# A second level of products over pairs of batches in the second layer of an attention and MLP kernel

## The chip, the cores and the metric

The kernel runs on one core of a Trainium2 chip. The metric is the device time of one execution in microseconds, as the median of several runs. All arithmetic is in float32; each 128-row float32 matmul of the program shows up as two matmul and two weight-load instructions in the trace.

## The reference, cut to what matters

```python
# q, k, v: (8 batches, 12 heads, 448 rows, 64);  w_in: (768, 2048);  w_out: (2048, 768)
q_n, k_n = rmsnorm(q, g_q), rmsnorm(k, g_k)          # x / sqrt(mean(x*x) + 1e-6) * g
attn = softmax(q_n @ k_n.T / 8)
x = (attn @ v)                                       # heads side by side: (8*448, 768)
h = x @ w_in
out = (h - tanh(h)) @ w_out                          # (3584, 768)
```

The weights come in as float64 and are rounded on the chip at the start.

## The kernel before

**Layout.** Everything is kept transposed: an activation tile has 128 features on the partitions and the 448 rows of one batch along the free dimension. A batch of the input of the first layer is six such tiles (`xT`, one for each pair of heads), its hidden activations are one tile of 16 blocks of 128 features (`gT`, `CF` = 16), its output six blocks.

**The two layers.** Batches 1 to 7 compute both layers with one level of the Winograd form of Strassen's scheme: rows are halved (2 x 224, `HS`), the inner and the outer features too, and seven half-size products replace eight. The weights' seven combinations are made once, during batch 0, and kept in scratch DRAM (`w_in_dram`, `w_out_dram`); from there they are loaded again for each batch into a ring of six slots in SBUF (`ring_load`, five ahead of use). The activations' combinations are `tt` (first layer, four GpSimd subtractions of 128x224 for a pair of `xT` tiles) and `tg` (second layer, `factors` at L838 to L840 and L872). Products come in the order `ORDER = (1, 5, 6, 2, 3, 7, 4)`; 2, 3 and 7 add to the PSUM banks of 1, 5 and 6, so that a bank is read out, added to by a product two later, and read again. Three PSUM banks (`mm`) serve the products in turn. `hidden(b)` is the first layer: four sets of seven products of six matmuls each; its results are read out by ScalarE and VectorE (L845 to L861), ScalarE takes the tanh (L827) and VectorE or GpSimd subtracts it (L828, "shrink"). `project(b)` is the second layer: three sets of seven products of eight matmuls. Batch 0 is different: its second layer is plain, 96 matmuls of 448 columns (L969), since the weights are still being rounded.

**Stores.** `store` transposes an output block in 32x32 pieces on VectorE into a buffer `th` (L886), of which there are two (ScalarE's tanh uses the same two), and after a few products SP issues its four transfers to DRAM (L891, `step_out`).

**Attention.** A step `s` is one pair of heads of one batch; there are 48. From step 13 on, a slot begins with a visit: TensorE computes the scores of step s+1 and the values of step s in 32-column pieces (L542, L608, L596), ScalarE takes the exponentials, and the result is divided into `xT` (L722 to L727). The helpers of later steps follow: for step s+1 VectorE adds up the exponentials (L573, L579, L586), transposes and reduces them (`fold` L683, `fold_rest` L690), ScalarE gathers the pieces (L698), VectorE and ScalarE spread the sums (`spread_sums`, `turn_sums`); for steps s+2 and s+3 the norms of q and k are made (`square_blocks`, `norm_blocks` L484, `meet_blocks`, and a power of -1/2 on GpSimd, L499), q and k are scaled (L506) and transposed (L516, L520), and `load_blocks` (L473) loads step s+4.

**Order.** There is no scheduler: each engine runs its instructions in the order in which the program issues them. The layers are a generator that yields after every matmul with a nominal time; `run(ns)` advances it. A slot runs the visit, then takes the list `work` of 14 points and advances the layers by an equal stretch before each point and after the last. `gap_ns` sets the length: before the change every slot from step 12 on gets a sixth of the two layers of one batch. The layers work on batch b-1 while the attention works on batch b, so the layers of batch 7 stand alone at the end.

Of the kernel before, what the change touches and what calls it, by code (L numbers as in the profile page):

```python
# [144 lines left out]
def bounded_path(tc, ctx, q, k, v, moe_w_in, moe_w_out, out, g_col, ident, ones, half_ones, neg_half, early):  # L145
# [32 lines left out]
    SETS = CF // 4  # L178
    ORDER = (1, 5, 6, 2, 3, 7, 4)
# [18 lines left out]
    gp = pool("gp", bufs=1)  # L198
    wp_stack = ctx.enter_context(ExitStack())
# [14 lines left out]

    def load(s, names):
        b, hp = steps[s]
        for name in names:
            src = {"q": q, "k": k, "v": v}[name]
            if s == 0 and name != "v":
                t = early[name]  # L220
            else:
                shape = [CP, 2, NCH, D] if name == "q" else [P, NCH, 2, D] if name == "k" else [P, 2, NCH, D]
                t = nat.tile(shape, F32, name=f"{name}_nat", bufs=3 if name == "v" else 2)
                fetch(nc, name, t, src[b, 2 * hp : 2 * hp + 2], in_order(s))
            loaded[name, s] = t
# [8 lines left out]
    BLOCKS = {1: 0, 2: 1, 4: 2, 7: 3, 5: 4, 6: 5, 3: 6}  # L234
    w_out_dram = scratch.tile([P, 7, HC, HF, P], F32, name="w_out")
# [151 lines left out]
    def ring_slot():  # L387
# [4 lines left out]
    ring_steps = [  # L392
        (b, layer, j, p)
        for b in range(1, B)
        for layer, count in ((0, SETS), (1, HC))
        for j in range(count)
        for p in ORDER
    ]
    ring_tiles = {}

    def ring_load(to):

        for n in range(len(ring_tiles), min(to, len(ring_steps))):
            b, layer, j, p = ring_steps[n]
            t = ring_tiles[ring_steps[n]] = ring_slot()
            if layer == 0:
                assert kept[1] > j
                nc.sync.dma_start(out=t[:, : 2 * HALF], in_=w_in_dram[j, p])
            else:
                nc.sync.dma_start(out=t, in_=w_out_dram[:, BLOCKS[p], j].rearrange("p f d -> p (f d)"))  # L410

# [53 lines left out]
    def load_blocks(s):  # L465
        b, hp = steps[s]
        t = loaded["qk", s] = late["blocks"].tile([P, 2, NJ, BL], F32, name="qk_nat", bufs=2)
        for i, src in enumerate((q, k)):
            for h in range(2):
                rows = src[b, 2 * hp + h].rearrange("(j t) (m d) -> m t j d", t=BL, d=BL)  # L470
                for m in range(2):
                    r = (2 * h + m) * BL
                    nc.sync.dma_start(out=t[r : r + BL, i], in_=rows[m])  # L473
# [19 lines left out]
    def power_blocks(s):  # L493
# [4 lines left out]
        normed["rr", s] = mine  # L498
        nc.gpsimd.tensor_tensor(  # L499
# [202 lines left out]
    def spread_sums(s):  # L702

        acc = whole[s]
        total = late["blocks"].tile([2 * BL, NJ], F32, name="sum_all")
        nc.vector.reduce_sum(total, acc.rearrange("p g j -> p j g"), axis=AX.X)
        nc.vector.reciprocal(total, total)
        wide = whole[s] = late["blocks"].tile([2 * BL, NJ, BL], F32, name="sum_w")
        nc.scalar.copy(out=wide, in_=total[:, :, None].to_broadcast([2 * BL, NJ, BL]))

    def turn_sums(s):

        wide = whole[s]
        rs = whole[s] = late["blocks"].tile([2 * BL, S], F32, name="rs_T")
        nc.vector.transpose(out=rs, in_=wide.rearrange("p j k -> p (j k)"))

    def divide(s, av):
        b, hp = steps[s]
        rs = whole.pop(s)
        x = xT[b, hp] = xp.tile([P, S], F32, name="xT")  # L720
        if s >= FOLDED:
            nc.scalar.copy(out=x, in_=av[0][:, :S])  # L722
            nc.vector.tensor_tensor(out=x, in0=x, in1=av[1][:, :S], op=ALU.add)  # L723
        for m in range(2):
            rows = slice(m * D, (m + 1) * D)
            if s >= FOLDED:
                nc.vector.tensor_tensor(out=x[rows], in0=x[rows], in1=rs, op=ALU.mult)  # L727
                continue
            for n in range(2):
# [6 lines left out]
        if hp < HC:  # L736
            return
        c = hp - HC
        if c == 0:
            tt[b] = tp.tile([P, 3, HC, HS], F32, name="tt", bufs=1)  # L740
        eng = nc.vector if b == 0 and c == HC - 1 else nc.gpsimd
        x11, x12, x21, x22 = (xT[b, r][:, n : n + HS] for r in (c, hp) for n in (0, HS))
        t1, t2, t4 = (tt[b][:, i, c] for i in range(3))
        eng.tensor_tensor(out=t1, in0=x12, in1=x11, op=ALU.subtract)
        eng.tensor_tensor(out=t2, in0=x22, in1=t1, op=ALU.subtract)  # L745
        eng.tensor_tensor(out=x12, in0=x22, in1=x12, op=ALU.subtract)
        eng.tensor_tensor(out=t4, in0=x21, in1=t2, op=ALU.subtract)
# [15 lines left out]
    def products(b, layer, count, width, depth, moving, done_with):  # L763
# [8 lines left out]
        def product(j, p, bank, first):  # L772
# [27 lines left out]
            for fn in now:  # L800
                fn()

# [9 lines left out]
    def hidden(b):  # L812

        g = late["g"] = gp.tile([P, CF, S], F32, name="gT")
        t2 = late["tg"].tile([P, 3, HF, HS], F32, name="tg") if b else None
        late["t"] = t2
        x = [xT.pop((b, c)) for c in range(CD)]
        t = tt.pop(b)
# [3 lines left out]
            4: lambda c: t[:, 2, c], 5: lambda c: t[:, 0, c], 6: lambda c: t[:, 1, c], 7: lambda c: x[c][:, high],  # L822
# [7 lines left out]
        def done_with(j):  # L830
# [11 lines left out]
            def use(p, bank):  # L842
                v = view(bank)
                if p == 1:
# [15 lines left out]
                elif p == 4:  # L860
                    nc.vector.tensor_tensor(out=s1, in0=v, in1=s1, op=ALU.add)  # L861

                    if b and j == SETS - 1:
                        factors()

                    def rest():
                        shrink(down, low, s1, nc.gpsimd)
                        if b and j < SETS - 1:
                            factors()
                        if b:  # L870
# [9 lines left out]
    def store(b, n, y):  # L880
# [15 lines left out]
        late["out"].append([2, issue])  # L896

    def step_out(by=1):
        for entry in late["out"]:
            entry[0] -= by  # L900
        while late["out"] and late["out"][0][0] <= 0:
            late["out"].pop(0)[1]()

# [35 lines left out]
    def project_first(b):  # L939
# [39 lines left out]
        late["tg"] = pool("tg", bufs=1)  # L979
        late["blocks"] = pool("blocks", bufs=1)  # L980

    def mlp():
        late["todo"], late["keep"], late["out"] = [], [], []
        for b in range(B):
            yield from hidden(b)
            yield from project(b) if b else project_first(b)
        for fn in late["todo"]:
            fn()
        step_out(2)
# [14 lines left out]
    O_NS = 4 * HS / ENGINE_NS * 7 * HC * HF  # L1004

    def gap_ns(s):
# [3 lines left out]
        return (H_NS + O_NS) / (4 * NP)  # L1010
# [72 lines left out]
    def slot(s):  # L1083
# [18 lines left out]

        def scale_or_turn():
            if first:
                turn(s + 2, sc_bank(), sc_bank())
            else:
                scale_blocks(s + 2)

        work = (
            ((rows, scale_or_turn),),  # L1110
            ((rows and not first, lambda: turn_blocks(s + 2, 0)), (first, lambda: load_blocks(s + 3))),
            ((rows and not first, lambda: turn_blocks(s + 2, 1)), (has(s + 4), lambda: load_blocks(s + 4))),
            ((following, lambda: add(s + 1, False)), (ahead and not first, lambda: square_blocks(s + 3))),
            ((following, lambda: add_third(s + 1)),),
            ((ahead and not first, lambda: norm_blocks(s + 3)),),
            ((following, lambda: add_last(s + 1)), (ahead and not first, lambda: meet_blocks(s + 3))),
            ((folded, lambda: fold(s + 1)),),
            ((folded, lambda: fold_rest(s + 1)), (first, lambda: square_blocks(s + 3))),
            (
                (folded, lambda: gather(s + 1, 0)), (ahead and not first, lambda: power_blocks(s + 3)),  # L1120
                (first, lambda: norm_blocks(s + 3)),
            ),
            ((folded, lambda: gather(s + 1, 1)), (first, lambda: meet_blocks(s + 3))),
            ((folded, lambda: spread_sums(s + 1)), (first, lambda: power_blocks(s + 3))),
            (),
            ((folded, lambda: turn_sums(s + 1)),),
        )
# [364 lines left out]
```

## Time and profile before

| | us |
|---|---|
| median of 3 runs | 1376.66 (1376.35 to 1377.57) |
| the profiled execution | 1375.42 |
| its span, first to last instruction | 1373.5 |
| TensorE matmul busy | 1344.5 |
| VectorE, ScalarE, GpSimd busy | 888.6, 551.1, 555.5 |

The granted clock of TensorE was 0.997 of full speed over the span. The span has three parts: up to 283 us the weights are rounded, the first batches' attention runs, and batch 0 goes through its layers; from 283 to 1217 us slots of 26.81 us follow each other; from 1217 to 1366 us the layers of batch 7 run alone. In the profile's lines "PE" is TensorE, "PEld" its weight loads, "DVE" VectorE, "ACT" ScalarE, "POOL" GpSimd and "SP" the engine that issues nearly all transfers. A line "L791 ... mm<-gT,w_f" is an instruction of line 791 that writes `mm` from `gT` and `w_f`.

### The profile page before, as it was taken

Reading aid. Unit: us, or ns where it says so; the run is one execution under the profiler, and the core shown is the slowest. Engines: PE = TensorE matmul, PEld = TensorE weight load, DVE = VectorE, ACT = ScalarE, POOL = GpSimd, SP = SyncE. Lnnn points to the kernel's source line nnn. Section 1 sums busy time; section 2 is a strip of 40 time slices with the busy share of each in tenths; the row PEclk is TensorE's granted clock in tenths of the full one; section 3 lists DMA queues with packets and bytes.
Section 4 is the critical chain, followed back from the end, with each engine's and each line's share of the span. In section 5 each row is a group of like instructions: output and inputs, shape, how many; then the busy total and the mean of one; then the engine's idle time right before and its main releaser. Section 6 shows DMA issues by size and latency. Waiting matters only on the chain.

```text
span 1373.5 us, 29906 instructions
## 1 busy us (share of the span) xinstructions
PE 1344.5 (98%) x11840; PEld 1126.3 (82%) x11840; DVE 888.6 (65%) x1378; ACT 551.1 (40%) x1314; POOL 555.5 (40%) x345
## 2 busy tenths in 40 slices
PE   7988999999999999999999999999999999999997
PEld 3466854479988998898899889889988998999997
DVE  5999989747855775666765578557765677533311
ACT  7855654344433444334433444334443344211100
POOL 4756665233632355315543336323463155302300
PEclk9999999999999999999999999999999999999999
DMA  7879889855675666666567657756665665556664
GB/s 167 193 201 259 252 257 248 252 147 148 208 191 135 181 186 186 150 163 197 168 164 202 163 142 203 191 146 160 196 188 155 159 196 164 143 161 183 191 190 91
DMA packets 367657, 249.91 MB, mean 182 GB/s; under 512 B 281748, under 2 KB 309780, under 8 KB 367508
## 3 DMA queue, kind: packets, MB, share of 16 engines
q1 hardware_dynamic: 367504, 247.90, 66.9%
q8 instruction: 96, 1.57, 0.5%
q14 instruction: 53, 0.43, 0.1%
q10 hardware_dynamic: 4, 0.00, 0.0%
HBM read 214.40 MB, written 33.42 MB: 180 GB/s over the span
## 4 chain that ended last, share of the span: by engine, by line
PE 93%; DMA 2%; SPq 2%; DVE 1%; ACT 1%; POOL 0%; issue 0%; ACTq 0%; POOLq 0%
PE mm L791 69%; PE sc L542 9%; PE sc L608 6%; PE mm L969 5%; PE sc L646 1%; PE sc L596 1%; DMA w_raw<-in_moe_w_in_dram 1%; PE mm L646 1%; SPq L272 1%; DMA gT<-in_moe_w_in_dram 0%; DMA w_in<-w_out 0%; PE mm L669 0%; PE sc L669 0%; SPq L125 0%; SPq L123 0%
## 5 line engine op out<-in xcount | busy, mean ns | idle before, releaser
L791 PE MATMUL mm<-xT,w_f 128*128 128x224 f32 x1392 | 275.6, 354 | 0.0
L791 PEld LDWEIGHTS mm<-xT,w_f 128*128 128x128 f32 x1392 | 262.1, 190 | 10.2 <-issue 9.5
L791 PEld LDWEIGHTS mm<-gT,w_f 128*128 128x128 f32 x1344 | 252.8, 190 | 12.8 <-issue 8.4
L791 PE MATMUL mm<-gT,w_f 128*128 128x224 f32 x1344 | 263.0, 354 | 0.0
L828 POOL TENSOR_TENSOR gT<-s,th 128x448 f32<-128x448 f32 x96 | 121.9, 1275 | 333.1 <-ACT th L827 329.4
L499 POOL TENSOR_TENSOR rr_mine<-rr_mine,neg_half 128x28 f32<-128x28 f32 x33 | 158.1, 4791 | 147.7 <-DVE rr_mine L497 96.8
L542 PE MATMUL sc<-qT,kT 64*32 64x448 f32 (+1 forms) x3072 | 213.7, 498 | 2.6 <-ACT p_last L548 1.7
L791 PE MATMUL mm<-tt,w_f 128*128 128x224 f32 x1044 | 208.6, 353 | 0.0
L791 PEld LDWEIGHTS mm<-tt,w_f 128*128 128x128 f32 x1044 | 197.1, 190 | 4.4 <-issue 4.4
L791 PE MATMUL mm<-tg,w_f 128*128 128x224 f32 x1008 | 197.5, 352 | 0.0
L791 PEld LDWEIGHTS mm<-tg,w_f 128*128 128x128 f32 x1008 | 190.7, 190 | 0.0
L542 PEld LDWEIGHTS sc<-qT,kT 64*32 64x32 f32 x3072 | 70.6, 106 | 70.4 <-issue 54.2
L723 DVE TENSOR_TENSOR xT<-xT,sc 128x448 f32<-128x448 f32 x35 | 21.7, 621 | 138.6 <-PE sc L542 94.9
L608 PE MATMUL sc<-p,v_nat 64*32 64x448 f32 x1120 | 110.5, 536 | 0.0
L745 POOL TENSOR_TENSOR tt<-xT,tt 128x224 f32<-128x224 f32 x23 | 30.3, 1317 | 168.0 <-DVE xT L727 147.3
L548 ACT ACTIVATE p<-sc 128x448 f32<-128x448 f32 x132 | 71.7, 543 | 48.2 <-PE sc L542 36.3
L827 ACT ACTIVATE th<-s 128x448 f32<-128x448 f32 x96 | 54.4, 573 | 69.3 <-DVE s L857 32.2
L698 ACT COPY sum_g<-sum 32x14 f32<-32x14 f32 x280 | 56.3, 201 | 55.1 <-DVE sum L690 43.7
L969 PE MATMUL mm<-gT,w_out 128*128 128x448 f32 x192 | 74.3, 542 | 0.0
L969 PEld LDWEIGHTS mm<-gT,w_out 128*128 128x128 f32 x192 | 35.7, 190 | 36.7 <-issue 36.4
L608 PEld LDWEIGHTS sc<-p,v_nat 64*32 64x32 f32 x1120 | 40.7, 107 | 29.9 <-issue 29.9
L142 POOL TENSOR_TENSOR rr<-rr,neg_half 112x8 f32<-112x8 f32 (+1 forms) x30 | 49.1, 1666 | 32.9 <-DVE rr L141 30.9
(151 smaller groups left out, 1819.5 us busy)
## 6 DMA issues: line engine op xcount, KB each, us to landing
w_f<-w_in SPq DMA_DIRECT2D x196, 384.0 KB, 3.6
w_f<-w_out SPq DMA_DIRECT2D x147, 512.0 KB, 4.5
w_raw<-in_moe_w_out_dram SPq DMA_DIRECT2D x16, 768.0 KB, 5.5
out_dram<-th SPq DMA_DIRECT2D x192, 56.0 KB, 3.6
w_in<-w_out SPq DMA_DIRECT2D x21, 384.0 KB, 5.3
qk_nat<-in_q_dram SPq DMA_DIRECT2D x132, 56.0 KB, 2.2
qk_nat<-in_k_dram SPq DMA_DIRECT2D x132, 56.0 KB, 2.3
v_nat<-in_v_dram SPq DMA_DIRECT2D x72, 96.0 KB, 4.1
```

The lines of the kernel that those rows point to most:

```text
L142: nc.gpsimd.tensor_tensor(out=r, in0=r, in1=neg_half[:rows], op=ALU.pow)
L499: nc.gpsimd.tensor_tensor(out=mine, in0=mine, in1=neg_half[:, :1].to_broadcast([P, 2 * NJ]), op=ALU.pow)
L542: nc.tensor.matmul(tiles[h][i * BL : (i + 1) * BL, :n], lhsT=kT[r, c * P + at : c * P + at + BL], rhs=qT[r, first : first + n], start=True ...
L548: nc.scalar.activation(p[:, h, c if c < 2 else 0, :], tiles[h][:, :n], AF.Exp, scale=1.0 if rr is None else rr[:, 0, 2 * c + h : 2 * c + h ...
L608: nc.tensor.matmul(av[g][i * BL : (i + 1) * BL, :S], lhsT=v_nat[keys, h, c, m * BL : (m + 1) * BL], rhs=p[keys, h], start=first, stop=True ...
L646: nc.tensor.matmul(av[n][r : r + BL, :HS], lhsT=v_nat[:, h, c, m * BL : (m + 1) * BL], rhs=p[c][:, h, n * HS : (n + 1) * HS], start=False, ...
L698: nc.scalar.copy(out=acc[h * BL : (h + 1) * BL, g], in_=part[g * BL : (g + 1) * BL, h * NJ : (h + 1) * NJ])
L745: eng.tensor_tensor(out=t2, in0=x22, in1=t1, op=ALU.subtract)
L791: nc.tensor.matmul(bank[:, f * HS : (f + 1) * HS], lhsT=w[:, c * width + f, :], rhs=moving[p](c), start=(first and f == 0 and c == 0), sto ...
L827: nc.scalar.activation(th, h, AF.Tanh, bias=0.0, scale=1.0)
L828: eng.tensor_tensor(out=g[:, rows, cols], in0=h, in1=th, op=ALU.subtract)
L969: nc.tensor.matmul(bank[:, :S], lhsT=w_out_row(f, n // HC)[:, n % HC * P : (n % HC + 1) * P], rhs=g[:, f, :], start=(f == 0), stop=(f == C ...
```

## The change

Batches 2 to 7 go through the second layer in pairs (2 and 3, 4 and 5, 6 and 7). The first level of the scheme now takes the two batches as the two halves of the rows: seven outer products (`OUTER = (1, 2, 3, 7, 6, 5, 4)`), each of 448 rows, 8 blocks of hidden features and 3 blocks of output features. Of each outer product, two of the three output blocks are computed with a second level, again seven products of half the rows and half the hidden features (four matmuls of 224 columns each), and the third block plainly, with eight matmuls of 448 columns.

- **Inner weights.** `inner_steps` makes the second level's weight sums while batch 1 goes through its layers, one step at each product: for each of seven outer products it fetches four blocks of w_out's combinations, makes four sums of 128x512 on GpSimd, and writes seven blocks to `inner_dram`. The ring then loads five tiles for an outer product (512, 512, 512, 256 and 512 KB).
- **Activation sums.** Outer sums (`outer_sum`, 16 a pair, 128x896, VectorE, in place) combine the two batches' hidden activations; inner sums (`inner_sum`, 4 for an outer product, 128x896, GpSimd, four buffers `u`) combine halves within. `factors` and `tg` remain for batch 1 only.
- **Output sums.** `combine_outer` adds the outer products' results into two accumulators (`acc`, `acc2`); part of these adds and all stores go to a list `calm`, from which one entry is taken at each product (two at some of the last outer product).
- **Order of the parts.** First layer of the even batch; two outer products (1 and 2), which need the even batch only; first layer of the odd batch; the other five outer products. `gap_ns` puts 4, 2, 4 and 2 slots beside these parts; the layers run six matmuls ahead of the slots (`AHEAD_NS`). For the last pair the odd first layer and the five outer products stand alone at the end.
- **The slot's list.** The power comes at the start of a slot, in place of point 10 of the slot before; the adds and `fold` come first, then the scale (point 6), the transposes, `load_blocks` (point 9, it was point 3), `spread_sums`, and the norms of step s+3 last. The x differences (`tt`) of batches from 2 on are made at points 5 and 9 of the fifth and sixth slot in place of directly after the division. The sums are spread to 128 partitions by VectorE, so that one multiplication in place of two finishes the division.
- **Memory.** q and k rows of all kinds share one pool of two buffers; a tenth `xT` tile (`xT_more`) and a second `gT` (`g2`) are added; `g2` also holds the blocks of `inner_steps`.

```diff
+    PAIRED = 2
+    OUTER = (1, 2, 3, 7, 6, 5, 4)
+    SOON = 2
+    ring_steps = ring_order(1, 0, SETS) + ring_order(1, 1, HC)
+    for first in range(PAIRED, B, 2):
+        for b, outer in ((first, OUTER[:SOON]), (first + 1, OUTER[SOON:])):
+            ring_steps += ring_order(b, 0, SETS)
+            ring_steps += [(first, 2, p, part) for p in outer for part in (1, 2, 3, 4, 0)]
...
+    def inner_steps():
...
+            work = (
+                (s1, a21, a22, ALU.add), (s3, a11, a21, ALU.subtract),
+                (s2, s1, a11, ALU.subtract), (s4, a12, s2, ALU.subtract),
+            )
+            for n, (out, x, y, op) in enumerate(work):
+                yield lambda: nc.gpsimd.tensor_tensor(out=out, in0=x, in1=y, op=op)
+                if n == 1 and i + 1 < len(OUTER):
+                    fetch_outer(i + 1)
+            yield lambda: None
+            keep(i, 1, block(sums, 0, 2))
...
+    def inner_sum(p, i):
...
+        nc.gpsimd.tensor_tensor(out=u, in0=a, in1=z, op=ALU.subtract)
...
+    def project_pair(b, ks):
...
+        for k in ks:
+            p = OUTER[k]
...
+            for i, q in enumerate(ORDER):
+                ring_load(step + 5 + i // 2)
+                step_out()
...
+                yield from matmuls(bank, HS, lambda c: w[:, c], moving, first)
+                flush()
...
+            bank = mm_bank()
+            yield from matmuls(bank, S, lambda i: w[:, i], [rows(p, f, 1, slice(0, S))[:, 0] for f in range(HF)], True)
+            flush()
+            late["todo"].append(lambda p=p, v=bank[:, :S]: combine_outer(p, HC - 1, v))
...
+        for b in range(PAIRED, B, 2):
+            yield from hidden(b)
+            while late["inner"] is not None:
+                inner_step()
+            yield from project_pair(b, range(SOON))
+            yield from hidden(b + 1)
+            yield from project_pair(b, range(SOON, len(OUTER)))
...
-        return (H_NS + O_NS) / (4 * NP)
+        if s < 3 * NP:
+            return (H_NS + O_NS + AHEAD_NS) / (4 * NP)
+        n = (s - 3 * NP) % (2 * NP)
+        return (H_NS / 16, OUTER_NS * SOON / 8, H_NS / 16, OUTER_NS * (len(OUTER) - SOON) / 8)[(n > 3) + (n > 5) + (n > 9)]
...
+            ((following, lambda: add(s + 1, False)), (first, lambda: turn(s + 2, sc_bank(), sc_bank()))),
+            ((following, lambda: add_third(s + 1)), (first, lambda: load_blocks(s + 3))),
+            ((following, lambda: add_last(s + 1)), (first, lambda: load_blocks(s + 4))),
             ((folded, lambda: fold(s + 1)),),
+            ((folded, lambda: fold_rest(s + 1)), (True, lambda: x_sums_later(s, 0))),
+            ((scaled, lambda: scale_blocks(s + 2)),),
+            ((scaled, lambda: turn_blocks(s + 2, 0)), (folded, lambda: gather(s + 1, 0))),
+            ((scaled, lambda: turn_blocks(s + 2, 1)), (folded, lambda: gather(s + 1, 1))),
+            ((True, lambda: x_sums_later(s, 1)), (has(s + 4) and not first, lambda: load_blocks(s + 4))),
+            ((folded, lambda: spread_sums(s + 1)), (ahead, lambda: square_blocks(s + 3))),
             ((folded, lambda: turn_sums(s + 1)),),
+            ((ahead, lambda: norm_blocks(s + 3)),),
+            ((ahead, lambda: meet_blocks(s + 3)),),
+            ((ahead, lambda: meet_rest(s + 3)),),
```

## The prediction

> **What bounds the kernel now.** I read the page's busy line first, then the chain of work that ended last, then the waits, then single lines.
>
> ```profile
> PE 1344.5 (98%) x11840; PEld 1126.3 (82%) x11840; DVE 888.6 (65%) x1378; ACT 551.1 (40%) x1314; POOL 555.5 (40%) x345
> ```
>
> TensorE is busy for 98%; a busy share says little of its rate, so the chain, in order of time (start, us, what):
>
> ```profile
> 260.40 12.22 PE mm L969 x32
> ...
> 496.07 21.38 PE mm L791 x112
> 517.45 0.54 PE sc L542 x16
> ...
> 522.88 2.28 PE mm L791 x11
> ```
>
> From 283 us to 1217 us it is the same piece over and over, and after that matmuls alone: 112 matmul instructions of the two layers in 21.38 us, 190.9 ns each, then one attention visit, and 26.81 us later (522.88 - 496.07) the next. Each matmul of the program is two instructions, so a 224-wide one costs 381.8 ns. The 448-wide ones of L969 take 12.22/32 = 382 ns an instruction; the pieces before (6.21 and 6.03 for 16) give the same mean, 382. Width changes nothing per column, and only the number of columns counts. The waits say that nothing else is on the path there (waiter, releaser, total, times, longest):
>
> ```profile
> PE mm L791 <- DVE s L847: 4.0, 2, 2.5
> ...
> SPq L473 <- DVE qk_n L506: 186.0, 31, 9.0
> ```
>
> TensorE's own waits are all before 283 us and small. SP stood up to 9.0 us in front of a load with the weight loads of the ring queued behind it, and no matmul waited: the ring hides that much.
>
> **What is removed on the path.** The order of TensorE's instructions has 2520 matmuls of 128x224 in the two layers before; after, 1512 + 588 of 128x224 and 168 of 128x448. So 420 x 0.3818 = 160.4 us go and 168 x 2 x 0.382 = 128.4 us come: -32.0 us. (At 388 ns, the slowest piece, it is -30.0.) Attention's matmuls stay as they are. With nothing else on the path until the end, this counts in full.
>
> **What is added beside it.** The layers' helpers need prices that the trace has only for other sizes. GpSimd subtracts 128x448 in 1.12 us and 128x224 in 0.66 us undisturbed, so 128x896 is about 2.06 us (at most 2 x 1.28 = 2.55, the mean with disturbance): 84 inner sums are 173 us; 28 sums of 128x512 about 35 us. VectorE gets 48 outer sums of 128x896 at 1.08 us (as L579), 52 us. For six batches the old factors go: 24 x (1.18 + 0.65) us of VectorE and 24 x (1.44 + 1.29) us of GpSimd. The spread of the sums moves from ScalarE (0.56 us) to VectorE; no such copy there, 0.3 to 0.63 us (L715), I take 0.5. The second multiplication of the division goes, 0.66 us a visit. All of this is off TensorE, and costs only where a product's bank is not read out in time. Three banks serve the products; a bank is needed again two products later: 4.6 us in the first layer, 6.1 us in the old second one, and now 2 x 4 x 0.382 = 3.05 us in the inner products.
>
> **The slots.** Beside the first layer a slot shrinks from 21.38 to 7 products = 16.04 us; beside two outer products to 16.8 us; beside the five it grows to 42 us. I walked VectorE's queue through the tightest, beside an odd first layer. Products end at 2.29, 4.58, 6.87, 9.17, 11.46, 13.75 and 16.04 us; the visit follows. In its own order, each at its row's duration less 0.08 us (neighbours overlap by that): division 1.2, add 2.2, read-out of product 5 2.9, two more adds 5.0, outer sum 6.0, product 6 6.6, transpose 7.6, reduce 8.6, scale 9.6, product 2 10.2 (its bank is due at 11.46), two transposes 11.3, product 3 11.8 (due 13.75), totals 13.0, product 7 14.1, transpose 14.7, norm 15.7, product 4 16.2. ScalarE, behind them, is free for the visit's exponentials at about 17.6; the first has to end by 16.04 + 1.9, when the visit's pieces (0.54, 0.75 and two of 0.33 us) come back to its bank. So it just closes, with 1.3 us to spare at product 2 and nothing at the visit. In an even layer all is 1 us earlier. What can eat the spare are GpSimd's subtractions:
>
> ```profile
> L838 DVE TENSOR_TENSOR tg<-gT x28: 553/1548/1576, 299.7 to 1303.0; 128x448 f32<-128x448 f32 x28
> ```
> ```profile
> L579 DVE TENSOR_TENSOR rows<-rows,p_full x35: 1074/1081/1849, 289.2 to 1199.9; 128x896 f32<-128x896 f32 x35
> ```
>
> (ns, least/median/most.) A VectorE instruction with both inputs in SBUF takes 0.55 us alone and 1.55 beside a GpSimd subtraction: the two take turns. A 2.06 us sum in front of such an instruction in the odd slot costs 2.06 - 1.3 = 0.8 us. That hits about one slot in four, and the outer products have little chance moments of the same kind (all but one pass my walk, with 0.2 us at the worst): 2.5 us in all. Bounds: 0, and over 1 us in each of 30 slots.
>
> The power is the exception among GpSimd's rows:
>
> ```profile
> 458.36 4.78 POOL L499 TENSOR_TENSOR rr_mine<-rr_mine,neg_half 128x28 f32<-128x28 f32 x1 [1.71 <-DVE rr_mine L497]
> ```
> ```profile
> 459.78 0.55 DVE L838 TENSOR_TENSOR tg<-gT 128x448 f32<-128x448 f32 x1
> ```
>
> Inside its 4.78 us the same L838 ran at its least. So I charge nothing for adds that now stand beside the power. The Trainium skill (GPSIMD Engine Reference, Key points) says that GpSimd shares its SBUF interfaces with VectorE's instructions of two SBUF inputs, with no such exception. Read so, the six slots beside two outer products, where the power runs late, would lose about 4.78 - 1.15 - 1.3 = 2.3 us each, 14 us, and the sum would be 1373 us. The row decides.
>
> The scale waits for the power, now 6 stretches after it. In the first slot beside the outer products GpSimd has 4.8 of power, four inner sums and two groups of x differences (2 x 4 x 0.66): 18.3 of 22.2 us, and the power still ends as the scale comes up. Its stall would fall on banks due only after the 6.1 us product, so 0.
>
> **Batch 1, making the inner weights.** Seven times 1.05 MB are fetched and 1.84 MB written: 20.2 MB in 45 of the 49 products, some 148 us. There the queues move
>
> ```profile
> 364.00:391.00 27.00, 27.00 (x243) 23.66 (x242) 15.70 (x27) 9.40 (x26) 12.08 (x8) 1.00 0.65 173
> ```
>
> 173 GB/s at a share of 0.65, 266 GB/s at full share: 20.2 MB need 76 us and 0.35 x 148 = 52 are free, 24 us short. At the best rate of any stretch (400 GB/s at 1.04 in 175 to 180 us) they need 50 us and fit. The ring hides about 9 us (above). So 0 to 15 us; I take 2, nearer the fast end, since these rows are of 2 to 8 KB as in that stretch, while of the packets in 283 to 445 us 37949 of 44240 are under 512 B. By the limit that the Trainium skill gives (DMA: Bandwidth & Descriptors, Specifications: about 358 GB/s of HBM for a core) the 173 + 136 GB/s would fit and the term be 0. SP also stands for GpSimd's sums in front of each write, less than the 9.0 us seen.
>
> **The outputs.** Each store transposes into one of two buffers, which is free again when its four transfers have landed: 0.65 us, four issues in 2.15 us, 3.3 us of landing. Before, stores came every 6 us or more:
>
> ```profile
> 1348.26 21.18 SPq L891 DMA_DIRECT2D out_dram<-th  x12
> ...
> 1365.98 0.39 DVE L932 TENSOR_TENSOR s<-mm,s 128x224 f32<-128x224 f32 x1 [2.34 <-PE mm L791]
> 1366.41 0.65 DVE L886 STREAM_TRANSPOSE th<-s 128x448 f32<-128x448 f32 x1
> ```
>
> The last matmul ended at 1365.98 and the span 7.5 us later, 6.4 of it after the last transpose. Now nine stores fall into the last outer product (16.8 us): every second waits for the one two before, 0.65 + 2.15 + 3.3 = 6.1 us. From its start the odd ones end at 5.6, 11.5, 17.6 and 23.7 us, then 6.4 us: 30.1, which is 13.3 after the last matmul. +5.8 us (bounds +0.6 for one more add alone, +10 with the longest landings of 4.9 us). At the two pairs inside the kernel the same bunch holds VectorE while the next batch starts, and ScalarE's exponentials behind it: about 1.5 us each, 3 us (0 to 5). In the last pair no visit covers the change from first layer to product 3; its second inner sum, behind two subtractions, comes about 1.5 us late (0 to 2).
>
> Loads of q and k move behind the scale, which takes their 186 us of SP waiting away; nobody waited for it, 0. The shared buffer for q and k, x differences later in the slot, other line orders: hidden by 5 to 17 us until use, 0; uncovered, a visit's 2 to 3 us once.
>
> **Sum.** -32.0 + 2.5 + 2 + 5.8 + 3 + 1.5 = -17.2 us. The profiled execution took 1375.42 us (span 1373.5), so 1358.2; the median of the runs lies 1.24 above it: 1359.5 us. A measurement here can tell some 0.2% (2.75 us) from no change.
>
> **Rivals.** (1) VectorE behind GpSimd becomes the bound beside the layers: if the turns cost every one of the 30 slots 1.2 us instead of one in four 0.8, the term is 36 instead of 2.5: 1393 us. For: by full durations VectorE has 18.9 of the odd slot's 21.5 us, and nothing to spare at the visit. Against: the subtractions fall mostly late in the slot. It decides from 0.75 us a slot, 22.4 us in all, on. Chance 0.20. (2) The fetches of batch 1 hold up the ring to their bound, 13 us more or somewhat less: about 1368 us; chance 0.12. (3) Nothing waits, and the stores land in time: -32.0 + 0.6, 1345 us; 0.08, with the counts as sure as the order of instructions; that the products saved are not there is excluded by it. (4) Both (2) and half of (1), within 0.2%: 0.05. The forecast has 0.55. Faster: 0.55 + 0.12 + 0.08 = 0.75. The range leaves out most of (1) and the lower half of (3): 1346 to 1382.
>
> **What would show it.** Right: pieces of matmuls at 190.9 and 382 ns without waits in the chain, pieces of 16 us between visits, an end about 13 us after the last matmul with transposes waiting for transfers. Wrong: TensorE waits for VectorE's read-outs or ScalarE's exponentials of over 10 us in all, or for w_f between 283 and 440 us.

## The result and the profile after

The changed kernel takes 1406.7 us (median; 1405.19 to 1406.94), the kernel before 1376.51 beside it: a ratio of 1.0217, 95% interval 1.0202 to 1.0233. The forecast of 1359.5 us was 47 us too low, and of the wrong sign. The profiled execution is the one of 1405.19 us (span 1403.3).

The products saved are there: TensorE has 11336 matmul instructions for 11840, and between visits the stretches beside a first layer last 16.02 us, as forecast (16.04). Nearly all the rest is waiting. The busy line, then three lines of the list of waits (waiter, releaser, total us, times, longest):

```profile
PE 1340.1 (95%) x11336; PEld 1051.6 (75%) x11336; DVE 1014.8 (72%) x1529; ACT 535.9 (38%) x1291; POOL 720.1 (51%) x409
```
```profile
ACT kT L547 <- DVE kT L546: 71.5, 31, 7.2
...
DVE sum_all L733 <- ACT sum_g L724: 30.2, 26, 1.6
...
PE sc L568 <- ACT p_last L574: 14.4, 12, 2.7
```

TensorE, which waited for nobody beside the layers before, now waits in the visits for ScalarE's first exponentials (more of this wait, 31.6 us, is booked on the weight loads). Where the time is, by the starts and lengths of the visits: before, every visit took 5.50 to 5.55 us; now 23 beside the pairs take 5.84 to 10.76 us, 33.7 us too much in all (13.9, 15.8 and 4.0 us in the three pairs). The two slots beside the five outer products hold 88.8 and 92.6 us of products for a count of 84: 4.8 and 8.6 us. Up to the end of batch 1 the kernel lost 1.1 us, the end of the span lies 13.4 us behind the last matmul (7.6 before), and some 8 us are small waits elsewhere. That is 62 us against 32 us of matmuls saved. About 5 of the 62 us are not waits but slower matmuls right behind two of them: the granted clock is 0.57 from 891 to 895 us and from 1051 to 1059 us.

One even slot, in order of time, shows how a visit comes to be late. First ScalarE, then VectorE in the same stretch (start, us, operation; in brackets the idle time before it and what ended it):

```profile
476.37 0.88 ACT L724 COPY sum_g<-sum 32x14 f32<-32x14 f32 x4 [0.67 <-DVE sum L716]
478.98 0.67 ACT L547 ACTIVATE kT<-kT,g_col 128x448 f32<-128x448 f32 x1 [1.73 <-DVE kT L546]
479.67 0.88 ACT L724 COPY sum_g<-sum 32x14 f32<-32x14 f32 x4
...
484.53 0.92 ACT L513 COPY rr_other<-rr_mine 32x28 f32<-32x28 f32 x4 [1.41 <-DVE rr_mine L506]
...
486.38 0.61 ACT L574 ACTIVATE p_last<-sc 128x224 f32<-128x224 f32 x2
```
```profile
478.35 0.60 DVE L546 STREAM_TRANSPOSE kT<-qk_n 128x448 f32<-128x448 f32 x1
...
480.58 0.24 DVE L733 TENSOR_REDUCE sum_all<-sum_g 64x14 f32<-64x56 f32 x1 [1.13 <-ACT sum_g L724]
...
483.46 1.04 DVE L506 TENSOR_REDUCE rr_mine<-qk_n 128x28 f32<-128x896 f32 x1
```

ScalarE's eight gathers are split four and four, and between them stands the multiplication of kT, which waits for VectorE's transpose of kT. So VectorE waits 1.13 us at the totals for gathers that have had their data since 476.4 us. All that VectorE does after that is 1.1 us later, the norm (L506) last. Behind the norm ScalarE makes the copies between lanes (L513), then a tanh and a read-out (0.58 and 0.51 us), and only then the exponentials that the visit, begun at 484.12 us, needs.

### The profile page after: what moved, and what is told of

Same layout as the page of the kernel before. It is cut to its first block, busy times and chain, and to the rows that moved or that the text cites. A ratio compares the mean times of both kernels' runs of the same rounds, so it can differ in the third digit from the quotient of the medians.

```text
span 1403.3 us, 29144 instructions
## 1 busy us (share of the span) xinstructions
PE 1340.1 (95%) x11336; PEld 1051.6 (75%) x11336; DVE 1014.8 (72%) x1529; ACT 535.9 (38%) x1291; POOL 720.1 (51%) x409
## 4 chain that ended last, share of the span: by engine, by line
PE 65%; DVE 16%; DMA 6%; issue 4%; SPq 4%; ACT 3%; POOL 2%; DVEq 0%; ACTq 0%; POOLq 0%
PE mm L832 26%; PE mm L1082 20%; PE sc L568 8%; PE mm L1246 5%; PE sc L634 4%; DMA out_dram<-th 2%; DMA qk_nat<-in_q_dram 1%; DVE qk_n L532 1%; DVE rows L605 1%; DMA w_f<-w_inner 1%; DVE rr_mine L506 1%; DMA gT<-in_moe_w_in_dram 1%; PE sc L672 1%; SPq L945 1%; DVE w_out L354 1%
## 5 line engine op out<-in xcount | busy, mean ns | idle before, releaser
L832 PEld LDWEIGHTS mm<-xT,w_f 128*128 128x128 f32 x1296 | 244.5, 190 | 10.2 <-DVE s L1089 5.4
L880 POOL TENSOR_TENSOR gT<-s,th 128x448 f32<-128x448 f32 x60 | 73.4, 1225 | 193.7 <-ACT th L879 193.7
L1082 PE MATMUL mm<-u,w_f 128*128 128x224 f32 x672 | 138.8, 358 | 4.6 <-DVE acc L1089 2.3
L1082 PEld LDWEIGHTS mm<-u,w_f 128*128 128x128 f32 x672 | 126.9, 192 | 13.5 <-issue 11.9
L880 POOL TENSOR_TENSOR g<-s,th 128x448 f32<-128x448 f32 x36 | 45.8, 1275 | 171.2 <-ACT th L879 171.2
L1082 PE MATMUL mm<-gT,w_f 128*128 128x224 f32 (+1 forms) x480 | 131.6, 427 | 0.0
L634 PE MATMUL sc<-p,v_nat 64*32 64x448 f32 x1120 | 130.9, 544 | 0.0
L1082 PEld LDWEIGHTS mm<-gT,w_f 128*128 128x128 f32 x480 | 90.9, 190 | 34.7 <-issue 34.0
L1082 PE MATMUL mm<-g,w_f 128*128 128x224 f32 (+1 forms) x360 | 100.7, 433 | 5.7 <-DVE s L1089 5.7
L1082 PEld LDWEIGHTS mm<-g,w_f 128*128 128x128 f32 x360 | 69.0, 193 | 33.7 <-issue 26.7
```

The lines of the kernel that those rows point to most:

```text
L634: nc.tensor.matmul(av[g][i * BL : (i + 1) * BL, :S], lhsT=v_nat[keys, h, c, m * BL : (m + 1) * BL], rhs=p[keys, h], start=first, stop=True ...
L832: nc.tensor.matmul(bank[:, f * HS : (f + 1) * HS], lhsT=w[:, c * width + f, :], rhs=moving[p](c), start=(first and f == 0 and c == 0), sto ...
L880: eng.tensor_tensor(out=g[:, rows, cols], in0=h, in1=th, op=ALU.subtract)
L1082: nc.tensor.matmul(bank[:, :n], lhsT=w(i), rhs=mv, start=(first and i == 0), stop=(i == len(moving) - 1), skip_group_check=not first,)
```

## The experiments

Four theories stand behind the expectations. A: the order of the engines' queues at a slot's end makes ScalarE late. B: GpSimd's subtractions hold VectorE. C: the slots are too short for their helpers. D: the stores' buffers. The kernel before took 1376.2 to 1376.6 us (median) beside all of them.

| | edit | us | against before (95%) |
|---|---|---|---|
| after | | 1406.7 | 1.0202 to 1.0233 |
| e1 | norm at the start of the slot | 1406.6 | 1.0202 to 1.0237 |
| e2 | one inner sum of four | 1384.9 | 1.0043 to 1.0077 |
| e3 | stores in place | 1400.4 | 1.0157 to 1.0191 |
| e4 | gather ahead of kT | 1378.6 | 1.0007 to 1.0027 |
| e5 | the helpers' old order | 1431.8 | 1.0387 to 1.0434 |
| e6 | e4, six of nine stores in place | 1373.1 | 0.9960 to 0.9985 |
| e7 | e6, x differences later | 1374.5 | 0.9975 to 0.9994 |
| e8 | e4, slots of even length | 1417.2 | 1.0277 to 1.0312 |
| e9 | e6, four outer sums later | 1363.4 | 0.9887 to 0.9917 |
| e10 | e9, first inner sum issued later | 1363.1 | 0.9891 to 0.9921 |
| e11 | e10 and e7 | 1365.5 | 0.9906 to 0.9934 |
| e12 | e9, first inner sum earlier, two queues for the last stores | 1351.4 | 0.9808 to 0.9835 |

**e4, one exchange of lines.**

```diff
-            ((scaled, lambda: turn_blocks(s + 2, 1)), (folded, lambda: gather(s + 1, 1))),
+            ((folded, lambda: gather(s + 1, 1)), (scaled, lambda: turn_blocks(s + 2, 1))),
```

> One exchange of lines: ScalarE's second gather stands in front of the multiplication of kT, which waits for VectorE's transpose. VectorE then no longer idles about 1.1 us at the totals in a slot, and the norm, which the visit waits for by way of ScalarE, comes that much earlier. Theory A, with this idle time as its main cause: 0.7 to 1.1 us in each of the 20 slots of 16 us that have such a visit, 10 to 20 us less: 1387 to 1397 us. If the copies behind the norm are late for another reason (VectorE full or held up, B or C), under 4 us: over 1402 us.

28 us less, more than expected. The visits' excess falls from 33.7 to 7.0 us; 8.9 us of this are the long visits of the first two pairs' fifth slots (see e2), which the expectation had not counted. ScalarE in the same slot:

```profile
477.21 0.67 ACT L547 ACTIVATE kT<-kT,g_col 128x448 f32<-128x448 f32 x1 [0.83 <-DVE kT L546]
...
483.38 0.61 ACT L574 ACTIVATE p_last<-sc 128x224 f32<-128x224 f32 x2
```

This visit began at 482.35 us: the exponentials start 1.03 us behind that, in the changed kernel 2.26 us (486.38 - 484.12). The transpose of kT still holds up ScalarE, but the gather that VectorE's totals need no longer stands behind it.

**e1, the norm moved.** `norm_blocks`, `meet_blocks`, `meet_rest` and the power go to the start of the next slot; scale, transposes and squares follow two to three points later, and the gathers come before them.

```diff
         if scaled:
-            power_blocks(s + 2)
+            norm_blocks(s + 2)
+            meet_blocks(s + 2)
```

> The norm, its four copies between lanes (ScalarE) and the power move from the end of a slot to its start, behind the visit's exponentials; the scale, the transposes and the squares move two to three stretches later. Theory A (order of the queues): the 26 visits beside the layers that are longer than 5.50 us (33.7 us in all) are late because ScalarE stands in front of these copies, which wait for VectorE's norm, with the tanh and the exponentials behind it. Then the visits are back at 5.5 to 6 us and the time falls by 25 to 34 us: 1373 to 1382 us. Theory B (VectorE held up by GpSimd's subtractions, whatever the order): VectorE comes as late to its read-outs as before, the time falls by less than 8 us: over 1398 us. Theory C (the slots of 16 us hold too much VectorE work): the stretch only moves, from the visits to the products at the start of a slot, again over 1398 us.

(The visits are 23, not the 26 named there.) No gain, and yet not theory B. The visits' excess falls by half, to about 15 us; what is left has another wait in the same place:

```profile
492.74 0.67 ACT L547 ACTIVATE kT<-kT,g_col 128x448 f32<-128x448 f32 x1 [3.64 <-DVE kT L546]
...
493.78 0.94 ACT L499 ACTIVATE qk_n<-qk_nat 128x896 f32<-128x896 f32 x1
...
496.03 0.61 ACT L574 ACTIVATE p_last<-sc 128x224 f32<-128x224 f32 x2
```

The kT multiplication now stands at the slot's end. It waits 3.64 us for VectorE, and a tanh, the squares and two more tanh stand between it and the exponentials. The first three slots of batch 1 also became some 9 us longer in all, and in the pairs some 17 us came back as waits of products for VectorE beside the first layers and the first two outer products. That is close to what theory C forecast for this run; what speaks against C is e4, where the same work fits into slots of the same length. This run couldn't tell the theories apart by its time, only by its lines.

**e5, the old order of helpers with the new products.** The list is that of the kernel before (scale, transposes, squares, norm, power in the middle, gathers and totals last).

> The pairs keep the new products, but the helpers beside them stand in the old order: scale and the two transposes first, squares, norm, its copies and the power in the middle of the slot, gathers and totals behind, with no transpose between the two gathers. Theory A (what was lost is ScalarE's place in the order at a slot's end, by whatever wait): no visit finds ScalarE behind the norm's copies or behind the kT multiplication, the visits go back to about 5.5 us, and the time is that of the exchange of lines (1378.6) or some us lower, 1370 to 1382 us. Theory C (a slot of 16 us holds too much for VectorE): the scale and the transposes, 2.3 us of VectorE right behind the visit, delay the first read-out and the adds, and the stretch goes on as waits of matmuls for VectorE: over 1390 us.

25 us slower than the changed kernel, out of both expectations. The visits take 7.8 to 12.1 us beside the first layers. GpSimd, then ScalarE, in front of one of them (it began at 486.63 us):

```profile
484.03 4.79 POOL L525 TENSOR_TENSOR rr_mine<-rr_mine,neg_half 128x28 f32<-128x28 f32 x1 [16.19 <-ACT sum_g L724]
488.78 3.31 POOL L880 TENSOR_TENSOR gT<-s,th 128x448 f32<-128x448 f32 x3
```
```profile
489.94 0.58 ACT L879 ACTIVATE th<-s 128x448 f32<-128x448 f32 x1 [3.37 <-POOL gT L880]
...
490.84 0.61 ACT L574 ACTIVATE p_last<-sc 128x224 f32<-128x224 f32 x2
```

GpSimd is in the power when the slot ends, its subtractions stand behind that, and ScalarE's third tanh waits 3.37 us for one of the two `th` buffers that these subtractions release. It is ScalarE in front of the exponentials again (theory A), by a wait that no expectation had named. In the kernel before, with 5.3 us more of products in each slot, such an order left every visit at 5.50 to 5.55 us.

**e2, fewer inner sums.**

```diff
+        if i:
+            us[p, i] = us[p, 0]
+            return
```

> Left out: three of the four inner sums of every outer product (63 of GpSimd's 84 subtractions of 128x896, some 2.06 us each undisturbed, 130 us); the first sum stands in for the others, so the output is not the reference's. TensorE's work is unchanged. Theory B (GpSimd's long subtractions hold VectorE): most of the stretch goes, 30 us or more: below 1377 us. Theory A (order of the queues): inner sums stand beside few visits, so only the two long visits of each pair's fifth slot (3.6 and 5.3 us too long) and the stalls of 1.5 to 2.9 us between products go: 10 to 18 us, 1389 to 1397 us. Theory D (the stores' two buffers make those stalls): 5 to 10 us, 1397 to 1402 us.

21.8 us less (with an output that is not the reference's): more than A expected, less than B. The lines say where: the two slots beside the five outer products fall to 83.3 and 83.9 us of products (from 88.8 and 92.6), and the long visits of the first two pairs' fifth slot (9.1 and 10.8 us) to 5.8. All other visits stay stretched. The fifth slot thus belongs to e4's gain and to e2's: the late gather makes VectorE late, and it then runs into the inner sums. VectorE and GpSimd there, in the changed kernel:

```profile
549.07 0.24 DVE L733 TENSOR_REDUCE sum_all<-sum_g 64x14 f32<-64x56 f32 x1 [1.64 <-ACT sum_g L724]
...
549.61 2.45 DVE L736 COPY sum_all<-sum_all 32x14 f32<-32x14 f32 x2
552.09 2.24 DVE L738 COPY sum_w<-sum_all 128x448 f32<-128x448 f32 x1
```
```profile
549.95 2.08 POOL L1040 TENSOR_TENSOR u<-gT 128x896 f32<-128x896 f32 x1
551.98 2.10 POOL L1040 TENSOR_TENSOR u<-gT,u 128x896 f32<-128x896 f32 x1
```

1.64 us late at the totals became some 5.6 us at the norm: the three copies take 0.75 us undisturbed and 4.69 here. In e2 VectorE still waits 1.64 us at these totals, but the copies take 0.75 us and the visit 5.76. In e4 these copies are through (1.14 us) before that pair of sums begins.

**e3 and e6, the stores.** e3 transposes every store of the pairs in place; e6 does so, on top of e4, only for the second accumulator and for product 4, which is summed in the accumulator.

```diff
-        o = part("th").rearrange("p f s -> p (f s)")
+        o = part("th").rearrange("p f s -> p (f s)") if b < PAIRED else y
```

In e6 the line is this one, and the stores of the second accumulator and of product 4 set `own`:

```diff
+        o = y if own else part("th").rearrange("p f s -> p (f s)")
```

> The stores of the pairs transpose in place and are sent from the product's own buffer, so that no transpose waits for one of the two shared buffers to land; nothing else is changed. Theory D (stores): VectorE's waits for landed transfers (31.8 us in 14 times) go, with them TensorE's stalls between products at the end of the first two pairs (4.8 and 8.6 us more than the count of matmuls gives) and the 5.8 us of the tail: 15 to 19 us less, 1388 to 1392 us. If the stalls between products come from GpSimd's subtractions (theory B), only the tail's share goes: 4 to 6 us, about 1401 us. In theory A the visits keep their 33.7 us in either case.

> On top of the exchange of lines of e4 (1378.6 us): the last product's stores and those of the second accumulator transpose in place, six of the nine at the end of a pair, the other three keep the two shared buffers. Theory D: the second slot beside the five outer products (43.6 and 45.9 us between visits) falls to the 41.6 us that e3 and e2 showed, 6.3 us, without e3's later waits for the ring, and the tail loses 3 to 5 us: 1367 to 1371 us. If the waits there come from SP's queue (transfers issued one after another) and not from the buffers: 0 to 3 us, 1375 to 1379 us.

e3 gave 6.3 us, about what theory B named, but not in the place that B named: its tail stayed at 13.8 us. The second slot beside the five products is free of waits in both (41.62 us between visits; before e3 it was 43.4 and 44.3); the first one, 45.3 us, is not, so this half of the waits is not the stores'. e3 pays part back in weights that come late in the next layer (1.1 and 1.9 us). e6 took 5.5 us off e4, between its two expectations: the second slot fell to 41.62 us as theory D says, but the tail, 13.5 us behind the last matmul, did not shrink, since SP's queue and not the buffers ends it (see e12).

**e7, e8, e9: the waits beside the outer products.** In e6 TensorE waits 2.85 us at the start of product 6, in each of the first two pairs. TensorE, then VectorE there:

```profile
707.61 3.33 PE L1082 MATMUL mm<-g,w_f 128*128 128x224 f32 x8 [2.85 <-DVE s L1089]
```
```profile
703.30 2.96 DVE L1032 TENSOR_TENSOR gT<-gT,g 128x896 f32<-128x896 f32 x1
706.18 1.07 DVE L506 TENSOR_REDUCE rr_mine<-qk_n 128x28 f32<-128x896 f32 x1
707.18 0.67 DVE L1089 TENSOR_TENSOR s<-mm,s 128x224 f32<-128x224 f32 x2
```

The read-outs (707.18), one of which TensorE's next matmul waits for, stand behind the adds of product 7 (one of them 2.06 us), an outer sum of 2.96 us (beside an inner sum) and a norm. e7 takes the x differences off GpSimd in this slot, e9 moves the outer sum:

```diff
-            6: {1: (3, 0), 6: (3, 1), 3: (3, 2), 4: (3, 3)},
+            6: {3: (3, 0), 4: (3, 1)},
+            5: {1: (3, 2), 5: (3, 3)},
```

> On top of e6: in the first slot beside the five outer products GpSimd no longer has the two groups of x differences (8 of 128x224, 3 to 6 us of it); they move into the second of these slots, where GpSimd idles. Theory B (GpSimd's queue and VectorE's turns with it make the waits of 2.85 us at 703 and 1023 us of e4): these waits shrink or go, 3 to 6 us less than e6. If they come from the inner and outer sums alone, which the order of the products fixes: within 1 us of e6.

> On top of e6: the four outer sums that only product 4 needs leave the start of product 6, where VectorE still has the adds of product 7 in its queue; two stand later in product 6 (behind products 3 and 4 of it), two at the start of product 5. Theory B': the waits of 2.85 us at 705 and 1026 us of e6 are VectorE's backlog at that place, made of outer sums of 1.0 to 3.0 us beside GpSimd's inner sums. Then both waits fall below 0.5 us, and with them the stretches of a lower granted clock right behind them: 6 to 10 us less than e6, 1363 to 1367 us. If the backlog only moves to product 5, the waits come back there: within 2 us of e6 (1371 to 1375 us).

e7 missed: the waits grew to 3.24 us. e9 took both away (the slot falls from 47.1 and 48.6 us between visits to 42.6) and 9.7 us of time. TensorE at the same place in e9, with no wait in front:

```profile
703.71 3.42 PE L1083 MATMUL mm<-g,w_f 128*128 128x224 f32 x16
```

e8 gives all slots of a half pair the same length:

```diff
+        return (H_NS + OUTER_NS * (SOON if n < 6 else len(OUTER) - SOON)) / 24
```

> On top of the exchange of lines of e4 (1378.6 us): the twelve slots of a pair are spread evenly over its two halves, six of 16.3 us and six of 24.7 us, instead of 4, 2, 4 and 2 beside the four parts; the products are the same. Theory C (the division into 4, 2, 4 and 2 leaves too little room in the odd layer's slots): the last stretched visits there (2 us a pair) go, and nothing else: 1373 to 1376 us. Theory B: more of the helpers then stand beside the five outer products, where VectorE and GpSimd already hold each other up, the waits of 2.85 us grow or multiply: 1379 to 1388 us.

38.6 us slower than e4, far beyond the worse expectation. The slots of 24.7 us are calm in the first layer (visits of 5.50), but VectorE's slot work now lies beside the outer products: waits of 4.93 and 4.82 us for VectorE in each of the first two pairs, and the third slot's visits take 8.6 to 10.2 us. So the uneven division into 4, 2, 4 and 2 slots is not what makes the change slow; the even one is worse.

**e10, e11, e12: the rest.** e10 issues the first inner sum later, e12 earlier (`(SETS // 2, 6)` becomes `(SETS // 2, 2)` or `(SETS // 2, 1)`); e12 also splits the last stores:

```diff
+                last = b == B - 1 or b == B - 2 and n >= HC
+                queue = nc.scalar if last and i % 2 else nc.sync
```

> On top of e9: the first inner sum of products 1 and 3, issued beside the third set of a first layer, moves from behind product 6 to behind product 2 of that set, 2.3 us later, where VectorE has a transpose and a reduction of one input. If GpSimd's turns with VectorE's two-input adds make the visits of 6.5 us that e6 still has in the third slot of each even layer (and part of those of 6.0 and 6.5 us in the odd ones): 1 us in each of three to five visits, 3 to 5 us less than e9. If a GpSimd subtraction holds VectorE's one-input instructions too: within 1 us of e9.

> On top of e10: the late x differences of e7. In e7 they made the wait in front of product 6 longer (3.24 for 2.85 us) but the start of the next pair shorter (16.0 for 17.3 and 18.5 us between visits). With the outer sums moved, the first should be gone and the second stay: 2 to 4 us less than e10. If the start of the next pair varies for another reason (the queue of stores and loads on SP): within 1 us of e10.

> On top of e9, two edits in stretches of the trace that lie far apart. First, the first inner sum of products 1 and 3 is put in GpSimd's queue in front of the power instead of behind it (e10's place was no later in time than e9's, since GpSimd was idle: the sum started right behind the power at 490.02 us). The sum then runs while the visit keeps VectorE idle, and the add right behind the visit (2.97 us in e10) falls to 1.1: if that add makes VectorE late at the next visit, the visits of 6.50 us in the third slot of an even layer fall to 5.5, three times 1 us, and those of an odd layer by part of 1 us each: 3 to 5 us. If not, the visits keep 6.5. Second, half of the transfers of the last pair's last six stores are issued from ScalarE's queue: in e10 SP issues the last 16 transfers in 10.32 us, one after another, and the span ends 13.9 us behind the last matmul. If SP's issue is what ends last, the tail falls to 8 to 10 us, 4 to 6 us less; if the landing in DRAM is, it stays. Both: 1354 to 1357 us; none: 1363.

e10 changed nothing, because the sum did not move: in e9 and in e10 it stands behind the power in GpSimd's queue and starts as soon as the power ends (491.30 and 490.02 us), so the point of issue does not decide its time. e11 was no faster: the start of the next pair, where it was to gain, was already at 16.02 us in e10, and its product 6 waits 0.3 us where e10's did not. In e12 both edits did what they should. GpSimd and VectorE in e10, then GpSimd and VectorE in e12:

```profile
485.28 4.79 POOL L525 TENSOR_TENSOR rr_mine<-rr_mine,neg_half 128x28 f32<-128x28 f32 x1
490.02 2.13 POOL L1040 TENSOR_TENSOR u<-gT 128x896 f32<-128x896 f32 x1
```
```profile
490.14 2.97 DVE L599 TENSOR_TENSOR rows<-p 128x896 f32<-128x896 f32 x1
```
```profile
486.35 2.12 POOL L1042 TENSOR_TENSOR u<-gT 128x896 f32<-128x896 f32 x1
488.42 4.79 POOL L525 TENSOR_TENSOR rr_mine<-rr_mine,neg_half 128x28 f32<-128x28 f32 x1
```
```profile
491.21 1.08 DVE L599 TENSOR_TENSOR rows<-p 128x896 f32<-128x896 f32 x1
```

The sum runs while VectorE idles in the visit; the even layers' visits are 5.50 to 5.55 us throughout. The tail falls from 13.9 to 6.9 us behind the last matmul. e12 is 55 us faster than the changed kernel and 25 us faster than the one before, 1351.4 us, more than e12's expectation.

## Why the prediction was wrong, step by step

**The products: right.** 32 us of matmuls went, at 190.9 and 382 ns. That this counts in full "with nothing else on the path" was the condition, and it failed.

**The slots: wrong, and the cause.** The step that failed is the walk of VectorE's queue, and in it the totals. It put the totals into a list of durations, each "at its row's duration", as if VectorE only waited for products. It left out that the totals wait for ScalarE's second gather, that this stands behind the kT multiplication, and that this waits for VectorE: 1.13 us of idle time in an even slot. With it the norm ended 16.4 us into the even slot (484.50 - 468.10) where the walk gives 14.7 (15.7 in the odd slot, 1 us less in an even one); the other 0.6 us are durations taken a little too short. In e4, without the wait, it ends at 15.2 us (481.50 - 466.34). By the walk ScalarE is free for the exponentials at about 16.6 us in an even slot, with a limit of 17.94 for the end of the first; they ended at 18.9 (486.99 - 468.10), 0.95 us beyond the limit, and the visit is longer by 0.78. So the limit was right, and the time at which ScalarE reaches it was not; with so little to spare, each microsecond missed counts. 2.5 us were forecast; with the gather moved e4 gained 28.

**GpSimd's turns: half right.** A late VectorE meets GpSimd's sums, as the prediction's rows of turns say, but the walk took only instructions with two inputs in SBUF as prone to it. The three copies of `spread_sums`, priced at 0.5 us, take up to 2.0 and 2.2 us each. This, behind 1.64 us of waiting at the totals, is the fifth slot's 3.6 us in the first pair. In the second pair the copies take as long, and the excess of 5.3 us has 1.7 us of slower matmuls in it: the granted clock over that visit is 0.84, over the first pair's 1.00.

**The power: right.** It doesn't block: in e12 it runs from 488.42 to 493.21 us, and the add of two SBUF inputs at 491.21 us takes 1.08 us.

**The outer products: wrong.** "All but one pass my walk" left out what a batch of adds in front of the read-outs does when an outer sum is among them at 2.96 us; that stop cost 2.85 us and, in part of the executions, a lower clock after it. e9 shows it.

**Batch 1: near in size, by luck.** 1.1 us for 2, but no matmul of batch 1 waits for weights: 0.4 us are lost before 283 us, and 0.7 in the second slot, where matmuls wait for read-outs by VectorE and ScalarE. **The bunch of stores at a pair's end: right in size**: the slot that holds it takes 43.4 and 44.3 us between visits, and 41.62 without waits (e9), 4.5 us for two pairs; 3 were forecast, for the start of the next batch. The slot before it, charged with nothing, is 8.4 us longer than in e9 (42.6). **The odd layer's end in the last pair: wrong.** 1.5 us were forecast for the late inner sum; the matmuls behind that layer wait some 0.4 us (1314.06 and 1315.60 us). A wait of 2.0 us for VectorE stands earlier, at 1213.77 us in that pair's first two outer products; it was not forecast, and e12 still has it. **The tail: right in size, half right in mechanism.** The tail's +5.8 us was +5.9. The two buffers do make VectorE wait (31.8 us in 14 times), but with the buffers taken away SP's issuing of one transfer after another ends as late. In e10, then e12, the last transfers from the accumulator:

```profile
1345.49 10.32 SPq L945 DMA_DIRECT2D out_dram<-acc  x16
```
```profile
1336.16 9.41 SPq L947 DMA_DIRECT2D out_dram<-acc  x8
```

In e10 SP goes on issuing for 6.6 us after the last transpose (1349.16 to 1355.81); in e12, where ScalarE's queue takes half of them, for 1.0 us (1344.53 to 1345.57).

**The rivals.** Rival (1) had the right side: VectorE late at the visit in every slot, 36 us, 1393 us. Its place was right; its price, by chance, near the 33.7 us that the visits lost; its cause was only part of it: e2 takes away three quarters of the inner sums and leaves the stretched visits, e4 leaves the sums and takes the stretch away. It should have had more than a chance of 0.20, since the walk itself left nothing to spare.

## What to carry to other kernels

Walk all in-order queues together: an engine's sum of durations says nothing where two engines wait for each other in turn, and two lines whose order means nothing to the result can cost 2% of the kernel. When a slot gets shorter, list for each engine what stands in front of the first instruction that the critical engine needs, and what each of those waits for; where the sum just fits, price the miss, not the fit. An instruction moved to another point of issue runs at the same time if the same instruction still stands in front of it in its engine's queue: to move it in time, change that order.

## What the runs showed of the hardware

**GpSimd holds VectorE's copies too.** The copy of 128x448 in `spread_sums` takes 394 ns in the median and up to 2248, and the small ones 168 and up to 2012; the transpose of the spread sums and the norm's reduction don't change (627 to 646 and 1041 to 1075 ns over the span). The Trainium skill (SBUF — State Buffer, SBUF: two separate sides) says that GpSimd and VectorE hold a shared port in turn, for the whole instruction, where VectorE's has two SBUF inputs or runs in a two-port mode, and it names the float32 copy as one that does. The rows agree for the copies; the power is an exception in every run here: VectorE's adds of 128x896 that start inside it take 1.07 to 1.09 us in the changed kernel, their time without GpSimd beside them.

**A short stop can halve TensorE's clock.** Groups of matmuls around the stop at product 6 of the second pair, in the changed kernel:

```profile
1047.83 1.68 PE L1082 MATMUL mm<-g,w_f 128*128 128x224 f32 x8
1052.36 3.35 PE L1082 MATMUL mm<-g,w_f 128*128 128x224 f32 x8 [2.85 <-DVE s L1089]
1055.50 4.68 PE L1082 MATMUL mm<-u,w_f 128*128 128x224 f32 x16
```

The granted clock there (stretch, length, busy time of the engines, clock, share and GB/s of the DMA):

```profile
1050.00:1055.00 5.00, 2.64 (x7) 2.43 (x8) 3.89 (x5) 1.19 (x5) 2.87 (x2) 0.67 0.64 161
1055.00:1060.00 5.00, 5.00 (x18) 4.47 (x17) 2.88 (x7) 0.00 (x0) 1.25 (x1) 0.65 0.20 52
```

After 2.85 us without work eight matmuls take 3.35 us for 1.68, and sixteen 4.68 for 3.19; the granted clock is 0.67 and 0.65 in these two stretches of 5 us, and 0.50 from 1052.3 to 1057.3 us. So the stop cost 2.85 + 1.67 + 1.49 = 6.0 us. In the first pair the same stop left the clock at 1.00, and e6's executions range from 1370.86 us (mean clock 0.996) to 1377.85 (0.990). The Trainium skill (TensorE: Matmul & The Clock Gate, What's actually happening) gives a free-running window of about 3.4 us without work before the clock falls; 2.85 us is less than that, and was enough in some cases. A stop of 2.01 us was enough in e9 (at 1173 us; clock 0.64 from 1174 to 1178 us) and not in e12 (at 1167 us; 1.00).
